# Top-k attention and a gated cosine feed-forward on one core: shared banks for scores and transposes, alternating feed-forward items, a shorter weight decode

## The chip, the cores and the metric

The kernel runs on one core of one Trainium2 chip. The core has TensorE (matrix products into the PSUM memory), VectorE, ScalarE and GpSimd (elementwise work), and SyncE, which here issues all DMA transfers. The metric is the device time of one launch in microseconds.

## The reference

For each of 8 batches and 8 heads, 576 queries of width 64 meet 576 keys. Only scores at or above the 32nd largest of a row take part in the softmax. The heads are put side by side to 4608 tokens of width 512, and a feed-forward block follows.

```python
scores = scale * np.matmul(q, k.transpose(0, 1, 3, 2))
kth = np.partition(scores, -top_k, axis=-1)[..., -top_k:-top_k + 1]
scores = np.where(scores >= kth, scores, -1000000000.0)
attn = np.exp(scores - np.max(scores, axis=-1, keepdims=True))
attn = attn / (np.sum(attn, axis=-1, keepdims=True) + 1e-09)
x = np.matmul(attn, v)          # then (B, H, S, D) -> (B*S, H*D)
h = x @ w_in                    # 512 -> 2048
out = (h * np.cos(h)) @ w_out   # 2048 -> 512
```

The weights arrive in 64-bit floating point; each is two 32-bit words, which the kernel turns into 32-bit floating point on the chip ("decoding").

## The kernel before

A **unit** is 128 tokens times one pair of heads; there are 36 x 4 = 144. For a unit, TensorE makes the scores (line 188) into the four PSUM banks of tag `sc`, and ScalarE copies them to the buffer `s` (line 198). VectorE finds the 32 largest of each row in four rounds of a MAX8 (line 212) for each head of the pair, with a replacement of the found values after the first three (line 215). GpSimd makes the bounds `nb` and `nd` from the largest and the 32nd (lines 222, 227), ScalarE masks with them (line 234) and takes exponentials with their row sums (line 242). GpSimd adds 1e-9 to the sums (line 249), VectorE takes the reciprocal (line 255), GpSimd normalises (line 260). TensorE transposes eight blocks of 128 x 128 (line 273) through two banks of tag `tp`, ScalarE copies them (line 274), a ninth, the tail, follows (lines 281, 282), and TensorE multiplies with the values (line 298), again into a `tp` bank. ScalarE puts the result into `xT`, the input of the feed-forward block (line 303).

The feed-forward block is cut into token blocks of 128 or 256. An **item** of the first product (`ff1`, line 344) gives 256 columns of `mm`; two fill a bank, four a `g` tile of 1024 columns. ScalarE evicts each bank (line 354). GpSimd reduces the argument of the cosine in three steps (lines 376 to 378) and a subtraction (line 385), ScalarE takes the sine (line 394), and GpSimd multiplies, the gate (line 401). In the last passes VectorE does GpSimd's part (lines 368, 371). An item of the second product (`ff2`, line 413) adds two of 16 slices of the hidden width; after eight items ScalarE evicts the bank (line 419) and SyncE writes 128 rows out. There are 288 items of each kind. Both products take their banks from tag `mm`, which has two.

Weights come in 32 chunks of 128 x 512, first 16 of `w_in`, then 16 of `w_out`. A chunk is loaded (line 102), taken apart by three ScalarE operations (lines 112 to 114), put together by three VectorE steps (lines 123, 124, 128), and finished by an addition and a multiplication on GpSimd (lines 131, 132).

The order of the work is written out by hand. The instructions of each engine run in the order of the program. The main loop (line 490) has one pass, a **slot**, per unit, and in slot `i` units `i` to `i - 3` are at different steps: `u` in its top-k rounds, `w` one unit behind in mask and exponentials, `x` two behind in normalising and transposes, `y` three behind in the product with the values. Scores are made one unit ahead. Feed-forward items are put between by `feed`, up to as many as a credit allows that grows by 4.3 a slot up to 6; it prefers the second product whenever the gates and all weights are ready. `decode` is called three times a slot, and a fourth time from slot 4 on. What is left of the feed-forward items after the last slot follows in a loop of its own (line 539). The first 12 units take their values one slot earlier.

## Time and profile before

| | us |
|---|---|
| median of 3 runs | 1827.48 (1827.01 to 1827.79) |
| the profiled execution | 1829.49 |
| its span, first to last instruction | 1827.4 |
| TensorE busy with products | 1614.0 (88%) |
| VectorE busy | 1492.9 (82%) |
| ScalarE busy | 1127.6 (62%) |
| GpSimd busy | 897.7 (49%) |

The mean granted clock of TensorE is 0.951 of full speed. "Busy" is the time in which an engine executes instructions; the product spans are partly modelled, and a busy TensorE may work at half the clock. A wait is put down to the engine and line that came last. In the rows, PE is TensorE, PEld its weight loads, DVE is VectorE, ACT is ScalarE, POOL is GpSimd, and L298 is line 298.

### The profile page before, as it was taken

To read this page: it belongs to the slowest core of one execution; us is meant where nothing else is said; L and a number is where in the kernel's file an instruction comes from. 1 tells how busy PE (TensorE), PEld (TensorE's weight loads), DVE (VectorE), ACT (ScalarE), POOL (GpSimd) and SP (SyncE) were. 2 spreads that over 40 slices of the span, in tenths; PEclk is the share of its full clock that TensorE was granted. 3 is DMA by queue.
4 is the path that set the end of the run, shared out by engine and by line. 5 is a ranking of instruction groups with operands and counts; after the bars stand their busy time and mean duration, and the time that the engine had idled before them with its cause. 6 is when DMAs were issued, how large, how long until landed. Compare 5 with 4: busy or idle time off the path is not lost.

```text
span 1827.4 us, 26780 instructions
## 1 busy us (share of the span) xinstructions
PE 1614.0 (88%) x9744; PEld 1098.3 (60%) x9744; DVE 1492.9 (82%) x3139; ACT 1127.6 (62%) x2022; POOL 897.7 (49%) x1128
## 2 busy tenths in 40 slices
PE   2464999899999898989899999999999999999997
PEld 1353757565747556565656566666666666666674
DVE  7999888989888889897979797879797978888421
ACT  5775575666665656666666666656666666667521
POOL 4787363363544536464646363645454545457200
PEclk9886999899999899999999999999999999999999
DMA  8430011002100020002000020001100010000000
GB/s 223 134 116 1 7 58 33 6 1 64 27 7 7 1 64 27 12 1 64 27 7 7 6 59 26 13 7 46 39 13 6 7 35 31 7 7 7 12 7 12
DMA packets 44227, 56.24 MB, mean 31 GB/s; under 512 B 10816, under 2 KB 27200, under 8 KB 44096
## 3 DMA queue, kind: packets, MB, share of 16 engines
q1 hardware_dynamic: 44096, 54.54, 9.9%
q8 instruction: 76, 1.25, 0.3%
q14 instruction: 55, 0.45, 0.1%
HBM read 45.09 MB, written 9.44 MB: 30 GB/s over the span
## 4 chain that ended last, share of the span: by engine, by line
PE 78%; ACT 8%; DVE 8%; POOL 3%; DMA 1%; issue 1%; SPq 0%; POOLq 0%; ACTq 0%
PE o L413 28%; PE mm L344 27%; PE o L298 9%; PE sc L188 8%; PE tp L273 5%; DVE m L212 2%; ACT x L394 2%; DVE rest L215 2%; ACT g L354 2%; ACT L394 1%; ACT pT L274 1%; POOL x L385 1%; ACT s L242 1%; PE tp L281 1%; DVE w_out L128 1%
## 5 line engine op out<-in xcount | busy, mean ns | idle before, releaser
L212 DVE MAX8 m<-rest 128x8 f32<-128x576 f32 x864 | 609.3, 747 | 0.0
L344 PE MATMUL mm<-xT,w_in 128*128 128x256 f32 (+1 forms) x2816 | 546.4, 346 | 25.0 <-ACT g L354 25.0
L413 PE MATMUL o<-w_out,g 128*128 128x512 f32 x1152 | 541.7, 612 | 17.5 <-POOL g L401 8.4
L344 PEld LDWEIGHTS mm<-xT,w_in 128*128 128x128 f32 x2816 | 447.4, 192 | 104.6 <-ACT g L354 38.4
L215 DVE MATCH_REPLACE8 rest<-m,rest 128x576 f32<-128x576 f32 x576 | 423.3, 742 | 0.0
L413 PEld LDWEIGHTS o<-w_out,g 128*128 128x128 f32 x1152 | 210.0, 194 | 267.5 <-issue 239.5
L249 POOL TENSOR_SCALAR den<-den 128x2 f32<-128x2 f32 x144 | 28.3, 196 | 667.6 <-ACT s L242 666.5
L212 DVE MAX8 m<-s 128x8 f32<-128x576 f32 x288 | 204.2, 750 | 129.6 <-ACT s L198 129.6
L234 ACT ACTIVATE s<-s,nb 128x576 f32<-128x576 f32 x288 | 207.9, 773 | 44.9 <-POOL nb L222 44.9
L354 ACT ACTIVATE g<-mm 128x512 f32<-128x512 f32 x144 | 85.4, 593 | 231.4 <-PE mm L344 231.4
L188 PE MATMUL sc<-k,q 64*128 64x288 f32 (+1 forms) x1280 | 201.5, 466 | 26.9 <-ACT s L198 15.8
L274 ACT COPY pT<-tp 128x512 f32<-128x512 f32 x288 | 153.8, 587 | 113.3 <-PE tp L273 113.2
L242 ACT ACTIVATE s<-s,nd 128x576 f32<-128x576 f32 x288 | 219.7, 765 | 0.5
L260 POOL TENSOR_SCALAR s<-s,rden 128x576 f32<-128x576 f32 x288 | 213.4, 752 | 0.4 <-DVE rden L255 0.4
L215 DVE MATCH_REPLACE8 rest<-m,s 128x576 f32<-128x576 f32 x288 | 211.6, 742 | 0.0
L273 PEld LDWEIGHTS tp<-ident,s 128*128 128x128 f32 x1152 | 137.8, 145 | 105.7 <-POOL s L260 53.8
L273 PE MATMUL tp<-ident,s 128*128 128x128 f32 x1152 | 157.6, 281 | 48.1 <-POOL s L260 45.2
L198 ACT COPY s<-sc 128x1152 f32<-128x1152 f32 x144 | 160.8, 1117 | 56.8 <-PE sc L188 56.6
L298 PE MATMUL o<-pT,v 128*64 128x128 f32 (+1 forms) x2560 | 179.9, 289 | 2.7 <-ACT pT L274 2.4
L298 PEld LDWEIGHTS o<-pT,v 128*64 128x64 f32 x2560 | 142.8, 150 | 58.5 <-ACT s L234 35.9
L401 POOL TENSOR_TENSOR g<-g,x 128x1024 f32<-128x1024 f32 x66 | 156.3, 2369 | 24.6 <-ACT x L394 24.6
L385 POOL TENSOR_TENSOR x<-g,x 128x1024 f32<-128x1024 f32 x66 | 156.6, 2373 | 5.3
(46 smaller groups left out, 1210.0 us busy)
## 6 DMA issues: line engine op xcount, KB each, us to landing
q<-in_q_dram SPq DMA_DIRECT2D x32, 288.0 KB, 3.1
out_dram<-ob SPq DMA_DIRECT2D x36, 256.0 KB, 2.0
st<-in_moe_w_in_dram SPq DMA_DIRECT2D x16, 512.0 KB, 5.2
v<-in_v_dram SPq DMA_DIRECT2D x32, 256.0 KB, 3.0
st<-in_moe_w_out_dram SPq DMA_DIRECT2D x16, 512.0 KB, 3.5
k<-in_k_dram SPq DMA_DIRECT2D x32, 144.0 KB, 3.3
k<-in_k_dram SPq DMA_DIRECT2D x32, 128.0 KB, 3.3
v_tail<-in_v_dram SPq DMA_DIRECT2D x64, 16.0 KB, 2.6
```

The costliest lines, as they stand in the source:

```text
L188: nc.tensor.matmul(sc[r0 : r0 + rows, j, h, 0:HS], st["q"][d, q0 : q0 + rows], st["k"][d, h * HS : (h + 1) * HS], start=True, stop=True,)
L212: nc.vector.max(m8[:, j, at], src[:, j])
L215: nc.vector.match_replace(rest[:, j], m8[:, j, at], src[:, j], NEG)
L234: nc.scalar.activation(out=s[:, j], in_=s[:, j], func=AF.Prelu, bias=nb[:, j, 1:2], scale=SCALE, alpha=FAR)
L242: nc.scalar.activation(out=s[:, j], in_=s[:, j], func=AF.Exp, bias=nd[:, j : j + 1], scale=1.0, accum_out=den[:, j : j + 1],)
L260: nc.gpsimd.tensor_scalar(out=s[:, j], in0=s[:, j], scalar1=rden[:, j : j + 1], scalar2=1.0, op0=ALU.mult, op1=ALU.mult,)
L273: nc.tensor.transpose(tp[:, c], s[:, j, k0 : k0 + P], ident)
L274: nc.scalar.copy(out=pT[:, :, j], in_=tp)
L298: nc.tensor.matmul(o[d, r], lhsT, rhs, start=c == 0, stop=c == NT)
L344: nc.tensor.matmul(mm[:, at : at + w], w_in[f // FC][:, c, (f % FC) * P : (f % FC + 1) * P], blk["xT"][:, c], start=c == 0, stop=c == NC - 1,)
L385: nc.gpsimd.tensor_tensor(out=x, in0=g, in1=x, op=ALU.subtract)
L413: nc.tensor.matmul(o, g[:, at : at + P], w_out[f], start=f == 0, stop=f == NF - 1)
```

## The change

The transposes of a unit go out together, the eight main ones into the four `sc` banks that the scores use, the tail into a bank `ot` that the product with the values uses as well; ScalarE copies all three afterwards. The second product has a bank `o2` of its own, so `mm` keeps its two for the first. `feed` alternates between the two kinds of items when both can go, with a credit of 3.7 a slot up to 5. Evictions of both products are not issued behind the last product of a bank but put on a list, which `take_banks` empties at two places of a slot. GpSimd's addition of 1e-9 becomes a VectorE operation ahead of the reciprocal, which moves to after round 2; normalising moves to the end of the slot before. Sines are taken only of tiles from an earlier slot. Chunks of weights are staged in the buffers of the `g` tiles (nine, not eight), taken apart in place, and decoded three a slot with two VectorE steps instead of three; GpSimd reads the staged words in place. An item waits only for the chunks that it needs. The first 8 units (before: 12) run their transposes and values early. In the main loop the loads of q, k and v stand behind the scores' copy, no longer at the start of the slot, `v` and `s` have a buffer less and `xT` one more, and the last two token blocks, not the last four, have 128 tokens. The diff, cut to its core:

```diff
-    CHUNKS, XB = 8, 4
...
-    def load_weights(i):
...
-        st = ffw.tile([P, CW, 2], I32, tag="x", name="st", bufs=XB)
...
-    def decode_first(i):
...
-        nc.scalar.activation(out=w, in_=hi.bitcast(F32), func=AF.Abs)
-        nc.scalar.sign(sg, hi)
-        nc.scalar.mul(out=r, in_=lo.bitcast(U32), mul=2.0**-29)
...
-    def decode_second(i):
...
-        nc.vector.tensor_scalar(out=w, in0=w, scalar1=2.0**-15, scalar2=None, op0=ALU.max)
-        nc.vector.tensor_scalar(
-            out=wi, in0=wi, scalar1=896 << 20, scalar2=3,
-            op0=ALU.bitwise_xor, op1=ALU.logical_shift_left,
-        )
-        nc.vector.tensor_scalar(
-            out=wi, in0=wi, scalar1=0x7FFFFFFF, scalar2=None, op0=ALU.bitwise_and
-        )
-        nc.gpsimd.tensor_tensor(out=wi, in0=wi, in1=r, op=ALU.add)
-        nc.gpsimd.tensor_tensor(out=w, in0=w, in1=sg, op=ALU.mult)
+    CHUNKS, XB = 9, 4
+    wq = {"next": 0, "loaded": deque(), "second": deque(), "done": 0, "ready": 0}
+
+    def load_weights(n):
+        for _ in range(n):
...
+            staging = len(wq["loaded"]) + len(wq["second"])
+            if staging >= 6 or staging + ff["live"] >= CHUNKS:
+                return
+            st = ffw.tile([P, CW, 2], I32, tag="g", name="st", bufs=CHUNKS)
+            nc.sync.dma_start(out=st.rearrange("p w i -> p (w i)"), in_=src)
+            wq["loaded"].append((st, dst))
+            wq["next"] = i + 1
+
+    def decode_first(n):
+
+
+        for _ in range(min(n, len(wq["loaded"]))):
+            st, w = wq["loaded"].popleft()
+            lo, hi = st[:, :, 0], st[:, :, 1]
+            nc.scalar.activation(out=w, in_=hi.bitcast(F32), func=AF.Abs, scale=2.0**16)
+            nc.scalar.sign(hi.bitcast(F32), hi)
+            nc.scalar.mul(out=lo, in_=lo.bitcast(U32), mul=2.0**-29)
+            wq["second"].append((st, w))
+
+    def decode_second():
+        for st, w in wq["second"]:
+            wi = w.bitcast(I32)
+            nc.vector.tensor_scalar(out=w, in0=w, scalar1=2.0, scalar2=None, op0=ALU.max)
+            nc.vector.tensor_scalar(
+                out=wi, in0=wi, scalar1=3, scalar2=None, op0=ALU.logical_shift_left
+            )
+
+    def decode_third():
+        while wq["second"]:
+            st, w = wq["second"].popleft()
+            wi = w.bitcast(I32)
+            nc.gpsimd.tensor_tensor(out=wi, in0=wi, in1=st[:, :, 0], op=ALU.add)
+            nc.gpsimd.tensor_tensor(out=w, in0=w, in1=st[:, :, 1].bitcast(F32), op=ALU.mult)
+            wq["done"] += 1
...
-        t = loads.tile([P, NT, P], F32, tag="v", name="v", bufs=6)
+        t = loads.tile([P, NT, P], F32, tag="v", name="v", bufs=5)
...
-        s = u["s"] = work.tile([P, 2, S], F32, tag="s", name="s", bufs=5)
+        s = u["s"] = work.tile([P, 2, S], F32, tag="s", name="s", bufs=4)
...
-    def add_eps(u):
-        den = u["den"]
-        nc.gpsimd.tensor_scalar(
-            out=den, in0=den, scalar1=1.0, scalar2=EPS, op0=ALU.mult, op1=ALU.add
-        )
-
     def reciprocal(u):
+        den = u.pop("den")
+        nc.vector.tensor_scalar(out=den, in0=den, scalar1=EPS, scalar2=None, op0=ALU.add)
         u["rden"] = small.tile([P, 2], F32, tag="rden", name="rden")
-        nc.vector.reciprocal(u["rden"], u.pop("den"))
+        nc.vector.reciprocal(u["rden"], den)
...
-    def transpose_main(u):
-
...
-        pT = u["pT"] = work.tile([P, NT, 2, P], F32, tag="pT", name="pT")
+    def transposes(u):
+
+        s = u.pop("s")
+        tp = u["tp"] = ps.tile([P, 2, 2, 512], F32, tag="sc", name="tp", bufs=1)
...
-            tp = ps.tile([P, NT, P], F32, tag="tp", name="tp")
-                nc.tensor.transpose(tp[:, c], s[:, j, k0 : k0 + P], ident)
-            nc.scalar.copy(out=pT[:, :, j], in_=tp)
-
-    def transpose_tail(u):
-
+                nc.tensor.transpose(
+                    tp[:, 0, j, c * P : (c + 1) * P], s[:, j, k0 : k0 + P], ident
+                )
+        tt = u["tt"] = ps.tile([P, 512], F32, tag="ot", name="tt", bufs=1)
+        nc.tensor.transpose(
+            tt[:, 0:P], s.rearrange("p j k -> p (j k)")[:, MAIN : MAIN + P], ident
+        )
+
+    def take_transposes(u):
+        tp, tt = u.pop("tp"), u.pop("tt")
+        pT = u["pT"] = work.tile([P, 2, NT * P], F32, tag="pT", name="pT")
+        for j in range(2):
+            nc.scalar.copy(out=pT[:, j], in_=tp[:, 0, j])
         pt = u["pT_tail"] = work.tile([P, P], F32, tag="pT_tail", name="pT_tail")
-        tp = ps.tile([P, 512], F32, tag="tp", name="tp")
-        s = u.pop("s").rearrange("p j k -> p (j k)")
-        nc.tensor.transpose(tp[:, 0:P], s[:, MAIN : MAIN + P], ident)
-        nc.scalar.copy(out=pt, in_=tp[:, 0:P])
+        nc.scalar.copy(out=pt, in_=tt[:, 0:P])
...
-        o = ps.tile([P, 512], F32, tag="tp", name="o")
+        o = u["o"] = ps.tile([P, 512], F32, tag="ot", name="o", bufs=1)
...
+
+    def take_values(u):
         blk = block_of[u["tok"]]
...
-        nc.scalar.copy(out=blk["xT"][:, u["hp"], at : at + P], in_=o[:, 0:P])
+        nc.scalar.copy(out=blk["xT"][:, u["hp"], at : at + P], in_=u.pop("o")[:, 0:P])
         blk["left"] -= 1
...
-    widths = [P] * 4 + [2 * P] * (B * S // (2 * P) - 4) + [P] * 4
+    widths = [P] * 4 + [2 * P] * (B * S // (2 * P) - 3) + [P] * 2
...
-        half = part // 2
+        full.append((take_first, blk, g, mm, part // 2))
+
+    def take_first(blk, g, mm, half):
         nc.scalar.mul(out=g[:, half * 512 : half * 512 + 512], in_=mm, mul=INV_2PI)
-        if half == 0:
-            return
-        fresh.append([blk, g])
+        if half == 1:
+            fresh.append([blk, g])
+
+    def take_banks():
+        while full:
+            take, *what = full.popleft()
+            take(*what)
...
-        if not waiting or (len(waiting) < least and waiting[0][3] + 2 > ff["now"]):
+        n = sum(c[3] < ff["now"] for c in waiting)
+        if n == 0 or (n < least and waiting[0][3] + 2 > ff["now"]):
             return
-        while waiting:
+        for _ in range(n):
...
-            blk["o"] = ps.tile([P, 512], F32, tag="mm", name="o2")
+            blk["o"] = ps.tile([P, 512], F32, tag="o2", name="o2", bufs=1)
...
+        full.append((take_second, blk, i, o))
+
+    def take_second(blk, i, o):
         ob = ffw.tile([P, DM], F32, tag="ob", name="ob")
         nc.scalar.mul(out=ob, in_=o, mul=2.0 * math.pi)
         row = blk["t0"] + i * P
         nc.sync.dma_start(out=out[row : row + P, :], in_=ob)
...
+    def can_first():
+        if not first:
+            return False
+        blk, i = first[0]
+        if blk["left"] or wq["ready"] < (((i + 1) * (256 // blk["w"]) - 1) // FC + 1) * NC:
+            return False
+        staging = len(wq["loaded"]) + len(wq["second"])
+        return i % 4 > 0 or ff["live"] + staging < CHUNKS
+
+    def can_second():
+        if not second:
+            return False
+        blk, i, f = second[0]
+        gated = sum(ff["tick"] >= t + 2 for t in blk["gated"])
+        return gated * 1024 // blk["w"] >= f + 2 and wq["ready"] >= NC * NF // FC + f + 2
+
     def feed(n):
 
         ff["tick"] += 1
         while n > 0 and ff["credit"] >= 1:
-            if second:
-                blk, i, f = second[0]
-                n_gated = sum(ff["tick"] >= t + 2 for t in blk["gated"])
-                if n_gated * 1024 // blk["w"] >= f + 2 and ff["weights"] == len(chunks):
-                    second.popleft()
-                    ff2(blk, i, f)
-                    n, ff["credit"] = n - 1, ff["credit"] - 1
-                    continue
-            if not first:
+            for kind in (ff["kind"], 1 - ff["kind"]):
+                if (can_first, can_second)[kind]():
+                    break
+            else:
                 return
-            blk, i = first[0]
-            need = (((i + 1) * (256 // blk["w"]) - 1) // FC + 1) * NC
-            if blk["left"] or ff["weights"] < need or (i % 4 == 0 and ff["live"] == CHUNKS):
-                return
-            first.popleft()
-            ff1(blk, i)
+            if kind == 0:
+                ff1(*first.popleft())
+            else:
+                ff2(*second.popleft())
+            ff["kind"] = 1 - kind
             n, ff["credit"] = n - 1, ff["credit"] - 1
-
...
-    for load, bufs, behind in ((load_qk, 5, -1), (load_v, 6, 4)):
+    for load, bufs, behind in ((load_qk, 5, -1), (load_v, 5, 3)):
         for n in range(NP, len(order)):
-            slot = last[order[n - bufs]] + behind if n >= bufs else 2
...
+    for hp in range(NP):
+        at_slot.setdefault(hp, []).append((load_v, 0, hp))
+    for hp in range(2, NP):
+        at_slot[hp - 2].append((load_qk, 0, hp))
+    EARLY = 2 * NP
     load_qk(0, 0)
-    load_weights(0)
+    load_weights(1)
+    load_qk(0, 1)
+    load_weights(2)
     scores(units[0])
     take_scores(units[0])
-    load_weights(1)
-    load_qk(0, 1)
-    scores(units[1])
-    decode()
-    take_scores(units[1])
-    for hp in range(2, NP):
-        load_qk(0, hp)
-    for hp in range(NP):
-        load_v(0, hp)
-    EARLY = 3 * NP
+    decode_first(3)
     for i in range(NU + 3):
         ff["end"] = i >= NU
         u, w, x, y = (units[i - n] if 0 <= i - n < NU else None for n in range(4))
+        early = w and i - 1 < EARLY
+        if x and i - 2 < EARLY:
+            x = None
+        if y and i - 3 < EARLY:
+            y = None
+        ff["credit"] = min(ff["credit"] + 3.7, 5.0)
+        ff["now"] += 1
+        wq["ready"] = wq["done"]
+        if w:
+            bounds(w)
+        if u:
+            if i > 0:
+                decode_second()
+            topk_round(u, 0)
+        take_banks()
+        if y:
+            values(y)
+        if i + 1 < NU:
+            scores(units[i + 1])
+        if y:
+            take_values(y)
+        if i + 1 < NU:
+            take_scores(units[i + 1])
         for load, b, hp in at_slot.get(i, []):
             load(b, hp)
-        ff["credit"] = min(ff["credit"] + 4.3, 6.0)
-        ff["now"] += 1
-        if w:
-            bounds(w)
-        if x:
-            normalise(x)
-        if u:
-            topk_round(u, 0)
-        decode()
+        gate(1)
         if w:
             mask(w)
             exponentials(w)
-        gate(1)
-        if w:
-            add_eps(w)
-        feed(1)
-        if y and i - 3 >= EARLY:
-            values(y)
-        if 0 < i < NU - 1:
-            scores(units[i + 1])
-            take_scores(units[i + 1])
+        if early:
+            reciprocal(w)
+            normalise(w)
         if u:
             topk_round(u, 1)
-        decode()
+            topk_round(u, 2)
+        if w and not early:
+            reciprocal(w)
+        feed(2)
+        take_banks()
+        if i > 0:
+            decode_third()
+            decode_first(3)
+        load_weights(3)
         reduce_first()
-        feed(2)
-        sines(2)
         if x:
-            transpose_main(x)
-        if u:
-            topk_round(u, 2)
-        decode()
+            transposes(x)
+            take_transposes(x)
+        feed(4)
+        if early:
+            transposes(w)
+            take_transposes(w)
+            values(w)
+            take_values(w)
         reduce_second()
-        feed(6)
-        if x:
-            transpose_tail(x)
-            if i - 2 < EARLY:
-                values(x)
+        if w and not early:
+            normalise(w)
         if u:
             topk_round(u, 3)
-        if i >= 4 and i < EARLY:
-            decode()
-        if w:
-            reciprocal(w)
-    while first or second:
+        sines(2)
+    while first or second or full:
         ff["now"] += 1
         ff["credit"] = 2.0
+        take_banks()
         gate(2)
         reduce_first()
         reduce_second()
```

## Rows read from the trace of the kernel before

**Rows 1.** Busy time by stretch, all engines: PE, PEld, DVE, ACT, POOL, clock, DMA.

```profile
8.65:193.84 185.19, 94.07 (x552) 68.37 (x553) 174.22 (x347) 118.97 (x219) 123.01 (x130) 0.82 0.36 107
193.84:415.02 221.18, 201.59 (x1436) 144.84 (x1435) 196.45 (x420) 140.22 (x260) 113.57 (x146) 0.93 0.08 24
415.02:1713.50 1298.48, 1214.16 (x7182) 813.41 (x7181) 1103.13 (x2353) 840.31 (x1497) 655.56 (x831) 0.97 0.07 22
1713.50:1827.40 113.90, 101.19 (x571) 69.92 (x569) 19.06 (x21) 25.68 (x46) 3.71 (x8) 0.97 0.03 10
```

**Rows 2.** The same of line 344 alone, then of line 413: PE, PEld, clock.

```profile
415.02:1713.50 1298.48, 408.98 (x1808) 320.43 (x1808) 0.97 0.07 22
1713.50:1827.40 113.90, 43.08 (x368) 42.26 (x368) 0.97 0.03 10
...
415.02:1713.50 1298.48, 424.65 (x902) 163.11 (x901) 0.97 0.07 22
1713.50:1827.40 113.90, 53.11 (x116) 21.75 (x114) 0.97 0.03 10
```

**Rows 3.** Timeline of PE over one slot: start us, us, engine, line.

```profile
1233.80 1.09 PE L298 MATMUL o<-pT,v 128*64 128x128 f32 x16
...
1236.21 3.70 PE L413 MATMUL o<-w_out,g 128*128 128x512 f32 x8
1239.75 1.04 PE L273 MATMUL tp<-ident,s 128*128 128x128 f32 x8
...
1244.31 1.89 PE L344 MATMUL mm<-xT,w_in 128*128 128x256 f32 x8
1246.14 1.09 PE L298 MATMUL o<-pT,v 128*64 128x128 f32 x16
```

**Rows 4.** Waits of 400 to 1700 us: us in total, times, longest.

```profile
DVE rden L255 <- POOL den L249: 88.2, 53, 6.1
...
PE tp L281 <- ACT pT L274: 52.6, 22, 4.3
...
PE mm L344 <- ACT g L354: 22.2, 36, 0.7
```

**Rows 5.** Busy time over two units that start without a wait.

```profile
318.24:337.64 19.40, 13.94 (x72) 8.95 (x71) 19.40 (x44) 14.32 (x24) 9.95 (x14) 0.60 0.00 0
```

**Rows 6.** Timeline of DVE, two decode steps.

```profile
129.98 0.42 DVE L123 TENSOR_SCALAR w_out<-w_out 128x512 f32<-128x512 f32 x1
...
136.62 2.44 DVE L128 TENSOR_SCALAR w_out<-w_out 128x512 int32<-128x512 int32 x1
```

**Rows 7.** Timeline of POOL over the same stretch.

```profile
134.97 1.33 POOL L132 TENSOR_TENSOR w_out<-w_out,lo_sg 128x512 f32<-128x512 f32 x1
136.26 2.52 POOL L385 TENSOR_TENSOR x<-g,x 128x1024 f32<-128x1024 f32 x1
```

**Rows 8.** Timeline of POOL in a slot at 801 us.

```profile
801.03 1.05 POOL L376 TENSOR_SCALAR x<-g 128x1024 f32<-128x1024 f32 x1 [0.29 <-ACT g L354]
...
804.43 2.36 POOL L385 TENSOR_TENSOR x<-g,x 128x1024 f32<-128x1024 f32 x1
...
807.21 1.48 POOL L260 TENSOR_SCALAR s<-s,rden 128x576 f32<-128x576 f32 x2
```

**Rows 9.** Timeline of ACT, mask and exponentials of one unit.

```profile
807.32 1.44 ACT L234 ACTIVATE s<-s,nb 128x576 f32<-128x576 f32 x2
...
808.78 1.28 ACT L242 ACT_TABLE_LOAD   x1
...
811.51 0.19 ACT L242 ACTIVATION_READ_ACCUMULATOR s<-s,nd 128x1 f32 x1
```

**Rows 10.** Costliest groups of the page: count, busy us, mean ns.

```profile
L354 ACT ACTIVATE g<-mm 128x512 f32<-128x512 f32 x144 | 85.4, 593 | 231.4 <-PE mm L344 231.4
...
L274 ACT COPY pT<-tp 128x512 f32<-128x512 f32 x288 | 153.8, 587 | 113.3 <-PE tp L273 113.2
...
L198 ACT COPY s<-sc 128x1152 f32<-128x1152 f32 x144 | 160.8, 1117 | 56.8 <-PE sc L188 56.6
```

More of the change, by code (lines that the diff above doesn't have):

```diff
@@ L90 @@
         chunks.append((moe_w_out[f * P : (f + 1) * P, :], w))
-    staged = {}
-    CHUNKS, XB = 8, 4
-    def load_weights(i):
-        if i >= len(chunks):
-            return
-        src, dst = chunks[i]
-        if not DECODE:
-            nc.sync.dma_start(out=dst, in_=src)
-            return
-        st = ffw.tile([P, CW, 2], I32, tag="x", name="st", bufs=XB)
-        nc.sync.dma_start(out=st.rearrange("p w i -> p (w i)"), in_=src)
-        staged[i] = [st]
-    def decode_first(i):
-        st = staged[i][0]
-        lo, hi = st[:, :, 0], st[:, :, 1]
-        w = chunks[i][1]
-        both = ffw.tile([P, 2, CW], F32, tag="g", name="lo_sg", bufs=CHUNKS)
-        r, sg = both[:, 0].bitcast(I32), both[:, 1]
-        nc.scalar.activation(out=w, in_=hi.bitcast(F32), func=AF.Abs)
-        nc.scalar.sign(sg, hi)
-        nc.scalar.mul(out=r, in_=lo.bitcast(U32), mul=2.0**-29)
-        staged[i] = [r, sg]
@@ new lines @@
+    ff = {"live": 0, "tick": 0, "now": 0, "credit": 0.0, "end": False, "kind": 0}
+    wq = {"next": 0, "loaded": deque(), "second": deque(), "done": 0, "ready": 0}
+    def load_weights(n):
+        for _ in range(n):
+            i = wq["next"]
+            if i >= len(chunks):
+                return
+            src, dst = chunks[i]
+            if not DECODE:
+                nc.sync.dma_start(out=dst, in_=src)
+                wq["next"] = wq["done"] = i + 1
+                continue
+            staging = len(wq["loaded"]) + len(wq["second"])
+            if staging >= 6 or staging + ff["live"] >= CHUNKS:
+                return
+            st = ffw.tile([P, CW, 2], I32, tag="g", name="st", bufs=CHUNKS)
+            nc.sync.dma_start(out=st.rearrange("p w i -> p (w i)"), in_=src)
+            wq["loaded"].append((st, dst))
+            wq["next"] = i + 1
@@ L294, in values @@
                     if c < NT:
-                        lhsT, rhs = st["v"][:, c, d], pT[:, c, j, r]
+                        lhsT, rhs = st["v"][:, c, d], pT[:, j, c * P + r0 : c * P + r0 + rows]
                     else:
@@ L318 @@
         t0 += w
-    ff = {"live": 0, "now": 0, "weights": 0, "credit": 0.0, "step": 0, "tick": 0, "end": False}
     first = deque((blk, i) for blk in blocks for i in range(2 * NF * blk["w"] // 512))
@@ L328 @@
     sined = deque()
+    full = deque()
     def ff1(blk, i):
```

23 lines of the change are left out of this document (3 added, 20 removed).

## The prediction

> **What bounds the kernel now.** The reading starts with busy time by stretch, cut where units 0, 12 and 32 start on VectorE and where unit 143 ends there [rows 1]. In the first stretch VectorE is busy 174.22 of 185.19 us and TensorE half of it: top-k search plus weight decoding is the limit, and TensorE lacks work. In the second TensorE is busy 201.59 of 221.18 us. In the third, 112 slots long, it is busy 1214.16 of 1298.48 us (93.5%) and VectorE 1103.13 (85%): TensorE sets the pace, 1298.48 / 112 = 11.59 us a slot. In the last only feed-forward work and the last units' attention are left. The granted clock is 0.82, 0.93, 0.97 and 0.97 of full speed (0.5 would be 1.2 GHz, 1.0 is 2.4 GHz), so TensorE loses time twice: idle, and then on the lower level.
>
> The second view counts feed-forward instructions in the last two stretches [rows 2]. Line 344 issues 16 to an item of a 128-token block and 8 to one of a 256-token block, line 413 issues 4. The last four blocks, of 128 tokens, have 512 of line 344, of which 368 lie in the last stretch; so the third holds 144 / 16 + (1808 - 144) / 8 = 9 + 208 = 217 items of the first product and 902 / 4 = 225 of the second: 442, or 3.95 a slot. The last holds 368 / 16 = 23 and 116 / 4 = 29: 52 items.
>
> The third view is TensorE's timeline over one slot without a wait, values to values [rows 3]: 1246.14 - 1233.80 = 12.34 us with four items of the second product and one of the first. Two of the second take 1239.75 - 1236.21 = 3.54 (1.77 each), one of the first 1246.14 - 1244.31 = 1.83. That leaves 12.34 - 7.08 - 1.83 = 3.43 us of attention (values, scores, transposes) in a slot. With 1.80 for a mean item, 3.95 items need 3.43 + 7.11 = 10.54 us where 11.59 are spent: about 1 us a slot, 118 over the stretch, is what can be won there.
>
> The waits of 400 to 1700 us name part of it [rows 4]: the tail transpose waits 52.6 us for the copy out of the main transposes' bank, the first product 22.2 us for its eviction. VectorE waits 88.2 us at the reciprocal. VectorE's own floor is a stretch of two units without idle time: 19.40 us, 9.70 a unit [rows 5].
>
> **The change part by part.** I price it by the same four stretches against the profiled execution (span 1827.4, its time 1829.49: 2.1 more). The median of the runs shown, 1827.48, is 2.0 under that execution, so a span that I work out stands nearly for a median as it is.
>
> Until unit 12. VectorE loses one decode step in three. A step takes 0.42 us at its fastest, and 2.44 where it starts during GpSimd's 2.52 us subtraction; a chunk's operation on GpSimd takes 1.33 [rows 6, 7]. The Trainium skill, SBUF — State Buffer, section "Who interferes with whom", says that a VectorE instruction in a two-port mode and GpSimd shut each other out of a shared port pair for a whole instruction. The trace agrees, with the 2.44 us. The new order puts six steps together at the start of a slot, when GpSimd may still add and multiply the chunks before. They cost 6 x 0.42 = 2.5 us at least and, each waiting for one chunk operation, 6 x 1.33 = 8.0 at most. I take 4.6, nearer the free row, since most of GpSimd's decoding lies beside the top-k rounds. A slot is then 9.70 + 4.6 = 14.3 us. Three chunks a slot (four were possible before) stretch decoding to slots 1 to 11. Unit 0 takes 9.7, a wait for the first weights 3, ten slots 143, one with two chunks 12.8. In slots 6 and 7 GpSimd's range reduction, 3.40 + 2.36 us [rows 8], stands between decoding and the next bounds; I let 4 us of each show, 8 together. ScalarE's nine decode operations in a row, ahead of the transposes' copies, may add 5. That is 181 us against 185.19: the saved step is largely spent on the slower rate of chunks. GpSimd's additions and multiplications now read every second word of the staged chunk, which no row shows: I take the old 1.33 us, nothing less, at most twice that, 8 us more of GpSimd a slot, of which some 5 would show. The bounds are 165 and 230.
>
> Units 12 to 31. Walking both queues through the new rules (credit 3.7 a slot, at most 5, nine buffers shared with staging, two ticks from gate to use) gives 20 items by slot 11 and 84 by slot 31: 64 items in 20 slots. TensorE needs 3.43 + 3.2 x 1.80 = 9.2 us a slot, less than VectorE's 9.70. Here VectorE is the bound. It gains the addition of 1e-9 that GpSimd did (128 x 2 elements), whose form no row shows: at least nothing, at most the 2.44 of a blocked step. GpSimd works about half the time, mostly in pieces of 1 to 2.4 us, so I take 0.4 on average. With 0.2 for uneven item supply a slot is 10.3: 206 us against 221.18, bounds 196 and 225.
>
> Units 32 to 143. The walk gives 494 items by slot 143: 410 in 112 slots, 3.66 each. TensorE needs 3.43 + 3.66 x 1.80 = 10.02, VectorE 9.70 + 0.4 = 10.1. Three waits of before lose their cause. All nine transposes go out together, so the tail no longer waits on the copy. The second product has its own bank, so both mm banks are free for the first while a sum is open. The reciprocal comes after round 2, by when the exponentials, early in ScalarE's slot, are through. What takes their place: the score banks now also hold the transposes, so scores wait for the transposes' copy and transposes for the scores' copy. Two items (3.6 us) cover the scores' copy of 1.12 us, as long as a slot has them; without them TensorE would pay it. From one values to the next, ScalarE's chain is 2.41 us (values and scores, 1233.80 to 1236.21), the scores' copy 1.12, mask to last accumulator read 4.38 (807.32 to 811.70, with a table load of 1.28; sines now come singly, so most slots have one), an eviction 0.59 and two copies 1.17 [rows 3, 9, 10]: 9.7 us, 0.3 under TensorE's slot. So a late mask is paid by TensorE.
>
> It is late where the range reduction waits for an eviction of the same slot. The accumulators then end at 2.41 + 1.12 + 3.10 (no load) = 6.6 us of the slot; eviction 0.59, reduction 3.40, subtraction 2.36, normalising 1.48 and bounds 0.42 (from 806.79 to 807.21) bring GpSimd to 14.9, which is 4.9 of the next slot [rows 8]. ScalarE was ready at 3.5 to 3.9, so the mask is 1.2 late, and 0.9 after the slack. A g tile comes every 2.2 slots, and in the walk some six in ten are such: 31 slots, 0.25 us on average. A slot is 10.1 + 0.3 = 10.4: 1165 us against 1298.48. Bounds: 9.9 and 11.4 a slot (the latter is the third rival).
>
> After unit 143. 576 - 494 = 82 items at 1.80 are 148 us, values and transposes of the last units 6. Before, 52 items (94 us) and some 6 us of attention took 113.9, so 14 us were lost. With items of both kinds alternating, 17 of the second product are left when the first runs out, 30 us of cover for the last gates. I take 6 us: 160, bounds 156 and 170. The late evictions cost nothing here or earlier: an eviction of 0.59 us has the next slot's values and scores ahead of its bank's reuse; without them TensorE would pay the 0.59. The loads move behind the scores' copy on the program's list but stay in order on SyncE's queue, where outputs and weights now stand ahead of them; a load into a q or k buffer waited for those same scores before, so I price the move at nothing. If it came later than the scores of the next slot, TensorE would wait.
>
> Sum: 8.65 (start to unit 0) + 181 + 206 + 1165 + 160 = 1721 us; I say 1722, 105 less than before.
>
> **The rivals.** A: nothing holds either engine in the long stretch. The slots run at TensorE's 10.0 us: 112 x 0.4 = 45 less, 1677. For it: VectorE's row at 9.70 without a break, and 0.3 us of slack in ScalarE's chain. Against it: blocked VectorE steps are in the trace.
>
> B: the moved addition is held behind GpSimd in most slots, as decode steps were, by half of the longest row, 1.2 us. VectorE then takes 9.70 + 0.1 + 1.2 = 11.0 a slot: 112 x 0.6 + 20 x 0.7 = 81 more, 1803. Against it: GpSimd is idle half the time. By the rule of the Trainium skill named above it can happen in any slot.
>
> C: slower. GpSimd becomes one chain with ScalarE: eviction 0.59, reduction 3.40, subtraction 2.36, normalising 1.48, bounds 0.42, mask to accumulator 4.38 make 12.6 us from one unit's exponentials to the next's [rows 8 to 10]. If every g tile meets it and nothing is caught up between, a slot averages (12.6 + 1.2 x 10.4) / 2.2 = 11.4: 112 more, 1834, slower than 1827.5. It decides from an average of 11.35 us on. Against it: in the slots between GpSimd has 3 to 4 us to spare.
>
> D: decoding gets slower: the six steps take 8.0 us, 10 x 3.4 = 34 more, or GpSimd's strided reads show 5 us in ten slots, 50 more: 1756 to 1772, still faster. Against it: GpSimd waits much in that stretch, 123 of 185 us busy [rows 1].
>
> **How the numbers follow.** The forecast gets 0.48, A 0.26, B 0.11, C 0.07, D 0.08. The range reaches from A with the early stretch at its lower bound (1677 - 16 = 1661) to just under B, 1800; left out are C, half of B and a little below A. 3.7 us, 0.2%, is about what a measurement of this kernel can tell from no change. Faster by more: 0.48 + 0.26 + 0.11 + 0.08 = 0.93, less 0.02 for cases of B that end at the old time: 0.91. Within: these 0.02. Slower: 0.07.
>
> **What would show it.** Right: units of the long stretch start 10.2 to 10.6 us apart on VectorE; the waits of the tail transpose and of line 344 for their copies are gone; TensorE is over 96% busy there at a granted clock near 1.0; about 160 us follow unit 143. Wrong: transposes or scores that wait for a ScalarE copy in most slots; the 128 x 2 addition with a mean near 1 us (B); the mask waiting for the bounds every second slot by 2 us or more (C); decode steps near 1.3 us or chunk operations near 2.6 (D).

## The result and the profile after

The changed kernel takes 1697.61 us (median of 4 runs, 1696.09 to 1698.95) against 1827.63 for the kernel before in the same comparison: a ratio of 0.9288, 95% interval 0.9272 to 0.9304. The forecast was 1722, with a range of 1661 to 1800. The profiled execution took 1698.95 us, its span is 1697.0, so spans again stand for medians within 2 us.

Busy time by stretch, cut at the same places (columns as in [rows 1], which these lines answer):

```profile
8.83:191.70 182.87, 106.66 (x667) 81.57 (x668) 172.27 (x327) 125.81 (x226) 128.72 (x122) 0.79 0.34 107
191.70:402.48 210.78, 187.57 (x1366) 133.06 (x1364) 200.31 (x442) 148.22 (x264) 104.72 (x125) 0.97 0.09 26
402.48:1543.70 1141.22, 1114.24 (x6932) 762.46 (x6932) 1120.76 (x2465) 856.03 (x1505) 605.89 (x705) 1.00 0.08 24
1543.70:1697.00 153.30, 147.97 (x653) 95.43 (x648) 30.25 (x31) 33.04 (x50) 3.59 (x5) 1.00 0.03 13
```

The stretches were forecast at 181, 206, 1165 and 160 us. Only the third is off by more than 7: 1141.22, or 10.19 a slot, where 10.4 was said. TensorE is busy 97.6% of it, VectorE 98.2%, at a granted clock of 1.00, the 2.4 GHz level (0.97 before).

The first and the second product's own lines, L355 then L431 [rows 2]:

```profile
402.48:1543.70 1141.22, 396.64 (x1656) 305.97 (x1656) 1.00 0.08 24
1543.70:1697.00 153.30, 63.61 (x392) 56.57 (x392) 1.00 0.03 13
...
402.48:1543.70 1141.22, 389.18 (x812) 146.29 (x812) 1.00 0.08 24
```

1656 / 8 + 812 / 4 = 410 items lie in the long stretch, as the walk of the queue said, 32 fewer than before. An item takes TensorE 1.78 us, the difference of two slots shown below. So the 157.3 us that this stretch lost divide in three: 32 x 1.78 = 57 are items put off to the tail (which grew by 39.4), 57 are idle time of TensorE (84.3 before, 27.0 now), and the other 43 are TensorE's own instructions. Some 29 of these are the clock: by the clock's records 65 us of the stretch's products ran at the lower level before and 7 us now, and from one product of line 413 to the next it is 853 ns there, 429 at the higher level. The last 14 were not traced.

The waits of 402 to 1543 us [rows 4]:

```profile
ACT s L243 <- POOL nb L231: 26.9, 28, 2.4
...
PE o L307 <- ACT pT_tail L291: 19.3, 21, 2.7
...
DVE den L258 <- ACT s L251: 16.2, 19, 1.2
...
PE tp L277 <- ACT s L207: 2.9, 2, 1.6
...
PE mm L355 <- ACT g L367: 0.3, 1, 0.3
```

The 52.6 us of the tail transpose and the 22.2 of the first product are gone (0.3 is left). Scores and transposes in common banks cost 2.9 us; no row has scores that wait for the transposes' copy. VectorE's wait at the softmax sums fell from 88.2 to 16.2.

TensorE's timeline, the starts of the values in four following slots [rows 3]:

```profile
750.85 1.09 PE L307 MATMUL o<-pT,v 128*64 128x128 f32 x16
...
759.62 1.09 PE L307 MATMUL o<-pT,v 128*64 128x128 f32 x16
...
771.38 0.88 PE L307 MATMUL o<-pT,v 128*64 128x128 f32 x12 [1.21 <-ACT pT_tail L291]
```

A slot with three items takes 759.62 - 750.85 = 8.77 us; the next, with four, 771.38 - 759.62 - 1.21 = 10.55 without its wait. VectorE's floor lies between the two, by its busy time over two units without a break [rows 5]:

```profile
710.88:730.69 19.81, 19.54 (x119) 12.90 (x116) 19.74 (x45) 15.75 (x27) 11.46 (x14) 1.00 0.04 14
```

That is 9.90 a unit, 0.20 over the old 9.70. From one unit's start on VectorE to the next there are 111 periods in the long stretch; 65 are at this floor (under 9.96) and 43 between 10 and 11. With the additions that were held (below) VectorE is busy 1120.76 / 112 = 10.01 us a slot, TensorE 1114.24 / 112 = 9.95: the two are nearly tied.

Two of the page's groups, the copies of scores and of transposes [rows 10]:

```profile
L207 ACT COPY s<-sc 128x1152 f32<-128x1152 f32 x144 | 161.2, 1120 | 127.4 <-PE sc L197 127.2
...
L289 ACT COPY pT<-tp 128x512 f32<-128x512 f32 x288 | 152.8, 582 | 17.4 <-PE tp L277 15.7
```

These copies cost what they did (1.12 and 0.58 us). Each waits mostly for TensorE's product.

### The profile page after: what moved, and what is told of

It is laid out like the page before. It is cut to its first block, busy times and chain, and to the rows that moved or that the text cites. A ratio compares the mean times of both kernels' runs of the same rounds, so it can differ in the third digit from the quotient of the medians.

```text
span 1697.0 us, 26520 instructions
## 1 busy us (share of the span) xinstructions
PE 1559.6 (92%) x9616; PEld 1074.2 (63%) x9616; DVE 1523.7 (90%) x3261; ACT 1165.5 (69%) x2046; POOL 844.8 (50%) x968
## 3 DMA queue, kind: packets, MB, share of 16 engines
q1 hardware_dynamic: 44096, 54.54, 10.4%
## 4 chain that ended last, share of the span: by engine, by line
PE 59%; ACT 16%; POOL 11%; DVE 11%; issue 2%; DMA 1%; SPq 0%; POOLq 0%; ACTq 0%
PE o L431 20%; PE mm L355 19%; PE o L307 8%; PE sc L197 8%; DVE m L221 5%; ACT s L251 5%; DVE rest L224 4%; PE tp L277 4%; ACT s L243 3%; POOL x L402 3%; ACT s L207 2%; POOL s L265 2%; ACT L251 2%; ACT pT L289 1%; POOL x L393 1%
## 5 line engine op out<-in xcount | busy, mean ns | idle before, releaser
L431 PE MATMUL o<-w_out,g 128*128 128x512 f32 x1152 | 548.5, 603 | 10.1 <-POOL g L419 7.0
L355 PE MATMUL mm<-xT,w_in 128*128 128x256 f32 (+1 forms) x2688 | 552.7, 353 | 0.3 <-ACT g L367 0.3
L355 PEld LDWEIGHTS mm<-xT,w_in 128*128 128x128 f32 x2688 | 446.9, 191 | 128.4 <-issue 89.8
L431 PEld LDWEIGHTS o<-w_out,g 128*128 128x128 f32 x1152 | 208.4, 191 | 197.5 <-issue 175.9
L307 PE MATMUL o<-pT,v 128*64 128x128 f32 (+1 forms) x2560 | 168.5, 277 | 55.8 <-ACT pT_tail L291 55.7
L307 PEld LDWEIGHTS o<-pT,v 128*64 128x64 f32 x2560 | 133.3, 142 | 133.9 <-ACT pT_tail L291 90.0
L197 PE MATMUL sc<-k,q 64*128 64x288 f32 (+1 forms) x1280 | 193.1, 449 | 11.6 <-DMA k<-in_k_dram 11.6
L277 PEld LDWEIGHTS tp<-ident,s 128*128 128x128 f32 x1152 | 138.2, 145 | 102.3 <-POOL s L265 52.6
L393 POOL TENSOR_SCALAR x<-g 128x1024 f32<-128x1024 f32 x63 | 66.2, 1050 | 205.8 <-ACT g L367 205.8
L314 ACT COPY xT<-o 128x128 f32<-128x128 f32 x144 | 37.9, 263 | 182.1 <-PE o L307 182.0
L419 POOL TENSOR_TENSOR g<-g,x 128x1024 f32<-128x1024 f32 x62 | 146.9, 2369 | 11.6 <-ACT x L412 11.6
L402 POOL TENSOR_TENSOR x<-g,x 128x1024 f32<-128x1024 f32 x63 | 149.3, 2370 | 5.3
```

The costliest lines, as they stand in the source:

```text
L197: nc.tensor.matmul(sc[r0 : r0 + rows, j, h, 0:HS], st["q"][d, q0 : q0 + rows], st["k"][d, h * HS : (h + 1) * HS], start=True, stop=True,)
L277: nc.tensor.transpose(tp[:, 0, j, c * P : (c + 1) * P], s[:, j, k0 : k0 + P], ident)
L307: nc.tensor.matmul(o[d, r], lhsT, rhs, start=c == 0, stop=c == NT)
L355: nc.tensor.matmul(mm[:, at : at + w], w_in[f // FC][:, c, (f % FC) * P : (f % FC + 1) * P], blk["xT"][:, c], start=c == 0, stop=c == NC - 1,)
L402: nc.gpsimd.tensor_tensor(out=x, in0=g, in1=x, op=ALU.subtract)
L431: nc.tensor.matmul(o, g[:, at : at + P], w_out[f], start=f == 0, stop=f == NF - 1)
```

## The experiments

All are edits of the changed kernel, run beside the kernel before. The slot is the mean of units 32 to 143, from VectorE's unit starts.

| kernel | us | ratio to before (95%) | slot, us |
|---|---|---|---|
| before | 1827.6 | 1 | 11.59 |
| after | 1697.6 | 0.9288 (0.9272 to 0.9304) | 10.19 |
| old banks | 1891.6 | 1.0346 (1.033 to 1.0361) | 11.58 |
| sum in `mm` | 1741.5 | 0.9523 (0.9509 to 0.9537) | 10.51 |
| second product first | 1765.5 | 0.966 (0.964 to 0.968) | 10.70 |
| credit 4.3 up to 6 | 1759.4 | 0.9619 (0.9599 to 0.9639) | 11.19 |
| credit 3.5 | 1755.6 | 0.9597 (0.9584 to 0.961) | 10.43 |
| credit 3.5, no addition | 1735.3 | 0.949 (0.9477 to 0.9503) | 10.23 |
| addition on GpSimd | 1722.3 | 0.9423 (0.941 to 0.9436) | 10.35 |
| three decode steps | 1711.8 | 0.9364 (0.935 to 0.9378) | 10.18 |
| evictions at once | 1705.1 | 0.9328 (0.9315 to 0.9342) | 10.22 |
| steps after round 0 | 1696.4 | 0.928 (0.9267 to 0.9292) | 10.18 |
| no addition | 1694.6 | 0.9272 (0.9259 to 0.9284) | 10.17 |
| no addition, steps after round 0 | 1692.4 | 0.9258 (0.9246 to 0.9271) | 10.18 |

**Which engine sets the pace?** The addition of 1e-9 is left out; the sums hold an exponential of zero, so they are 1 or more, and 1e-9 is lost in 32 bits anyway.

```diff
-        nc.vector.tensor_scalar(out=den, in0=den, scalar1=EPS, scalar2=None, op0=ALU.add)
```

> Leaves out the addition of 1e-9 to the row sums (the sums are at least 1). Theory M: in the long stretch (units 32 to 143, 10.19 us a unit after the change) VectorE's floor of 9.90 us and TensorE's need of 10.02 are nearly tied, and the addition, 0.15 us alone and up to 1.6 behind GpSimd, is what lifts VectorE over it. Without it VectorE's floor is 9.70, TensorE sets the pace at 10.05: 15 us less there, 5 in units 12 to 31, 2 before: about 1676 us against 1697.6. Rival T, TensorE or its chain with ScalarE sets the pace alone: 1693. Rival V, VectorE alone: its 39 us and the waits go in full, 1655.

Measured: 3 us less, near rival T (1693). VectorE's floor fell from 9.90 to 9.70 us, but the slot went from 10.19 to 10.17: the other slots became longer by what the short ones won (15 periods over 11 us, 2 in the changed kernel). TensorE, busy 9.95 and idle 0.24 a slot, sets the mean, and the theory of VectorE as the bound falls.

**The same with less work for TensorE.** Credit 3.5, with the addition and without:

```diff
-        ff["credit"] = min(ff["credit"] + 3.7, 5.0)
+        ff["credit"] = min(ff["credit"] + 3.5, 5.0)
```

> The changed kernel with one number altered: a slot's credit is 3.5 items, not 3.7. By the rules of the queue 390 items then fall into units 32 to 143 instead of 410, and 20 more follow unit 143. Theory: in the changed kernel TensorE paces the long stretch (9.95 us busy and 0.24 of waits a slot) with VectorE just under it (9.70 us and a mean of 0.27 for the moved addition, 9.97). With 20 items of 1.78 us less TensorE needs 9.63 + 0.24 = 9.87 a slot, so VectorE takes over at 9.97 to 10.05: 112 x 0.14 to 0.22 = 16 to 25 us are saved in the long stretch, 36 are added behind it, and the time is 1709 to 1718. Rival: VectorE's addition is hidden at any pace, slots follow TensorE down to 9.87, both ends cancel and the time stays within 1694 to 1702.

> The same credit of 3.5 and, besides, no addition of 1e-9 ahead of the reciprocal. Theory: without the addition VectorE needs 9.70 us a slot, TensorE's 9.87 sets the pace again, the long stretch saves about 36 us against the changed kernel and the tail adds 36: 1692 to 1699, that is 11 to 20 us under the kernel with the same credit and the addition (against 3 us at a credit of 3.7). Rival: the addition is hidden at this pace too, and the two kernels differ by 5 us at most.

Measured: the two differ by 20 us, at the upper end of what the theory said (11 to 20): at this rate VectorE's addition does show. But both are some 40 us slower than said. The long stretch of the first, with the addition:

```profile
400.70:1569.35 1168.65, 1103.15 (x6861) 751.00 (x6860) 1142.69 (x2465) 851.01 (x1499) 590.12 (x695) 0.98 0.08 23
```

By their instructions 393 items lie in it, 17 fewer than in the changed kernel. At 1.78 us they should have brought TensorE's busy time from 1114 to 1084; it is 1103. Some 15 of these 19 us are the clock (0.98; 37 us of products at the lower level, 7 in the changed kernel). TensorE idles 65.5 us, not 27. Waits in the stretch:

```profile
ACT s L243 <- POOL nb L231: 55.7, 48, 2.8
PE o L307 <- ACT pT_tail L291: 32.5, 27, 3.4
PE o L431 <- ACT ob L440: 26.2, 11, 4.2
```

The last two have grown by 38 us together, which is all the new idle time: the values wait longer, with 48 late masks and not 28, and the second product now waits for the eviction of its only bank (1.5 us in all in the changed kernel). VectorE is busy 1142.69 / 112 = 10.20 us a slot, 0.20 more than in the changed kernel, with as many instructions. The moved addition accounts for it, first here and then in the changed kernel's long stretch:

```profile
L258 DVE TENSOR_SCALAR den<-den 128x2 f32<-128x2 f32 x112 | 54.3, 485 | 22.1 <-ACT s L251 22.0
...
L258 DVE TENSOR_SCALAR den<-den 128x2 f32<-128x2 f32 x112 | 31.0, 277 | 16.6 <-ACT s L251 16.2
```

So the expectation was wrong in taking the changed kernel's waits (0.24 us a slot for TensorE, 0.27 for the addition) over to another rate. Whole numbers of items alone do not explain the miss. By the timeline 53 of the 112 slots have three items and 55 four. If three cost VectorE's floor of 9.90 and four TensorE's 10.55, the mean would be near 10.2. But from values to values TensorE takes 9.39 us for three and 11.23 for four, and the same sum would put the changed kernel (33 and 76 such slots) at 10.35, not 10.19: there a slot of three takes 9.07 us, so short slots do lend time to long ones. Why the waits grow at this rate was not traced further.

**More credit.**

```diff
-        ff["credit"] = min(ff["credit"] + 3.7, 5.0)
+        ff["credit"] = min(ff["credit"] + 4.3, 6.0)
```

> Credit 4.3 a slot up to 6 as before the change, everything else as after. Theory M: TensorE's work is the same in sum, so items that go earlier shorten the tail: slots of the long stretch take 10.6 to 10.7 us (TensorE alone sets the pace), the tail loses some 35 items of 1.8 us; the total stays within 10 us of 1697.6, between 1688 and 1708. Rival: the lower credit was the gain, as more items a slot bring back late masks and stalls: 1740 or more.

```profile
410.79:1663.67 1252.88, 1189.64 (x7108) 808.83 (x7109) 1114.11 (x2465) 844.58 (x1504) 637.22 (x724) 0.98 0.07 23
```

Measured: 62 us slower than the changed kernel. The long stretch is 112 us longer. By their instructions 444 items lie in it: the 34 that the tail no longer has (it is 57 shorter) are 60 of the 112, another 15 of TensorE's busy time go with the lower clock (0.98; 42 us of products at the lower level), and 36 are idle time (63.2 against 27.0). Units 12 to 31 add 9. A slot now gets anything from none to six items; by the queue's rules a higher credit empties the queue of finished gates and then waits for the next. VectorE waits for the softmax sums 86 times, not 19:

```profile
DVE den L258 <- ACT s L251: 134.9, 86, 6.2
```

The rival's number came, but not by late masks: there are 18 of them, fewer than the changed kernel's 28. Of the three rates run 3.7 is the best by far: 3.5 costs 58 us, 4.3 (with its cap of 6) costs 62.

**The banks.** The order of the changed kernel with the old banks: transposes, tail and values through the two of `tp`, the second product through `mm`.

```diff
-        tp = u["tp"] = ps.tile([P, 2, 2, 512], F32, tag="sc", name="tp", bufs=1)
+            tp = ps.tile([P, 512], F32, tag="tp", name="tp")
...
-        tt = u["tt"] = ps.tile([P, 512], F32, tag="ot", name="tt", bufs=1)
+        tt = u["tt"] = ps.tile([P, 512], F32, tag="tp", name="tt")
...
-        o = u["o"] = ps.tile([P, 512], F32, tag="ot", name="o", bufs=1)
+        o = u["o"] = ps.tile([P, 512], F32, tag="tp", name="o")
...
-            blk["o"] = ps.tile([P, 512], F32, tag="o2", name="o2", bufs=1)
+            blk["o"] = ps.tile([P, 512], F32, tag="mm", name="o2")
```

> As the run before, and the transposes go back into two banks of their own that the tail and the values share, as before the change; the order of the slot stays. Theory M: the tail transpose waits for the first copy again, about 1 us in each of 112 slots, so about 100 more than with only the sum moved: 1870. Rival: taking the score banks bought nothing by itself, since the order of the slot does the work: within 10 us of the run before.

```profile
DVE den L258 <- ACT s L251: 176.2, 94, 6.1
PE tt L283 <- ACT pT L291: 131.7, 110, 4.9
```

Measured: 194 us slower than the changed kernel, and slower than the kernel before. The tail transpose, now right behind the main ones, waits in 110 of 112 slots for the copy out of its bank; before it waited in 22, because items stood between [rows 4]. The new order needs the new banks; alone it is a loss.

Only the last of these edits, the second product back in `mm`:

> The second product's sum goes back into the two mm banks. Theory M: the bank of its own is what took TensorE's wait for evictions away. With the sum open most of the time, the first product has one bank, and since evictions are issued late it waits 1 to 2 us in about half of the slots: some 80 us more, about 1775, with the first product's wait for its eviction back in the list. Rival: the slack of TensorE and the alternation hide it: 1700.

```profile
DVE den L258 <- ACT s L251: 51.0, 41, 5.9
PE mm L355 <- ACT g L367: 30.2, 18, 4.3
```

Measured: 44 us slower, about halfway between the expectations. The first product waits for its evictions again, up to 4.3 us at a time where it was 0.7 before; that the evictions come later now would explain the longer ones, but this was not run apart. By difference the other 150 us of the test above belong to the places of the transposes, the tail and the values.

**Alternation.** The second product goes first whenever it can, as before the change:

```diff
-            for kind in (ff["kind"], 1 - ff["kind"]):
+            for kind in (1, 0):
```

> The second product is preferred again whenever it can go; no alternation. Theory M: the number of items a slot decides, not their kind; but a sum that ends and one that begins in the same feed share one bank and wait for a late eviction: 10 to 30 us more, 1708 to 1728. Rival: without alternation the last gates are not covered and first products come in bursts that wait for their two banks: 1750 or more.

```profile
DVE den L258 <- ACT s L251: 75.6, 53, 5.7
PE o L431 <- ACT ob L440: 39.8, 14, 4.8
```

Measured: 68 us slower, 57 of it in the long stretch and 11 behind unit 143. With sums back to back the one bank `o2` has to be evicted while TensorE wants it: 39.8 us of waits where the changed kernel has 1.5. The rival's bursts at the two `mm` banks cost only 3.4 us. At a credit of 3.7, alternation is what makes a single bank enough; at 3.5 the bank is waited for even so.

**Late evictions.** `take_banks()` behind every item:

```diff
             ff["kind"] = 1 - kind
+            take_banks()
```

> Evictions are issued right behind the item that fills a bank, no longer from the list. Theory M: ScalarE then stands before a product that TensorE has not finished, with the sines and the next slot's copies behind it; the mask starts later and TensorE pays in some slots: 20 us more, about 1717. Rival: ScalarE waits for TensorE at the scores anyway: within 5 us of 1697.6.

Measured: 7.5 us slower, between the two expectations. 4.8 of it lie in units 12 to 31, 3.2 in the long stretch.

**The place of the addition.** Back to GpSimd, behind the exponentials:

```diff
+            add_eps(w)
...
-        nc.vector.tensor_scalar(out=den, in0=den, scalar1=EPS, scalar2=None, op0=ALU.add)
```

> The addition of 1e-9 goes back to GpSimd, right behind the exponentials, as before the change; the reciprocal stays after round 2. Theory M: VectorE's floor falls to 9.70, but the reciprocal now waits for one more engine; 5 to 15 us less than 1697.6, between 1683 and 1693. Rival: moving the addition to VectorE was worth something by itself: 1710 or more, with the reciprocal waiting for GpSimd in most slots.

```profile
DVE rden L265 <- POOL den L258: 65.9, 61, 2.7
ACT s L243 <- POOL nb L231: 55.9, 44, 3.0
PE o L312 <- ACT pT_tail L296: 28.3, 30, 3.5
```

Measured: 25 us slower, and the way it takes shows a chain: the addition is late on GpSimd for VectorE's reciprocal in 61 slots, then the bounds (44 late masks, 28 in the changed kernel), then the values on TensorE (28.3 us, 19.3 in the changed kernel). Against the version without any addition, VectorE's costs 3 us and GpSimd's 28.

**The decode steps.** The old third step, an AND with 0x7FFFFFFF, put back:

```diff
+            nc.vector.tensor_scalar(
+                out=wi, in0=wi, scalar1=0x7FFFFFFF, scalar2=None, op0=ALU.bitwise_and
+            )
```

> A third VectorE step (an and with 0x7FFFFFFF, which changes nothing) is put back behind the two of each chunk. Theory M: VectorE is the bound until unit 12 and a step costs 0.86 us beside GpSimd: 32 x 0.86 = 27 us, of which 20 or more show: 1718 to 1725. Rival: the early stretch is held by GpSimd's and ScalarE's chains: within 5 us of 1697.6.

Measured: 14 us slower, 13.5 of it before unit 12, between the expectations. The 32 steps are 22.7 us of VectorE (77.9 in all against 55.2), so about three fifths of them showed.

The six steps behind top-k round 0 and not ahead of it:

```diff
         if u:
+            topk_round(u, 0)
             if i > 0:
                 decode_second()
-            topk_round(u, 0)
```

> The two VectorE decode steps of a slot's chunks are issued after top-k round 0, no longer before it. Theory M: the steps (mean 0.86 us after the change, 0.42 when free) are long because they meet GpSimd's chunk work of the slot before, which ends about when round 0 does. Their mean falls to about 0.5, VectorE loses 22 us of the 55 until unit 12, and half of that or more shows: about 1685. Rival: the early stretch is held by the chain of ScalarE's copies, products and exponentials: steps get shorter, the time stays within 3 us of 1697.6.

Two of its four groups of decode steps, on VectorE from 8 to 200 us:

```profile
L131 DVE TENSOR_SCALAR w_out<-w_out 128x512 int32<-128x512 int32 x16 | 15.3, 958 | 0.6
...
L130 DVE TENSOR_SCALAR w_in<-w_in 128x512 f32<-128x512 f32 x16 | 6.9, 434 | 0.0
```

Measured: the steps of `w_in` now run free (434 ns, 710 in the changed kernel), those of `w_out` do not; the mean of all is 0.69 us, not 0.5. VectorE saves 11 us, and the time moves by 1 us, inside its spread. VectorE's decoding is thus not alone in pacing the first slots. Together with the dropped addition the same edit gives the fastest version of all, 1692.4 us:

> Both edits together (the addition of 1e-9 left out, the decode steps after round 0). Theory M: they act in different stretches, so the gains add up: about 1664 us. Rival: the time won early is lost again at the end, as TensorE's work is the same: 1676, no more than without the addition alone.

Measured: 5 us under the changed kernel, all of it before unit 12 (177.5 us there, not 182.9), and neither 1664 nor 1676: both had counted on the 22 us that leaving out the addition did not give.

## Why the prediction was right, and where it was not

**The direction and the mechanism** held. The waits that were to vanish vanished, TensorE is 97.6% busy where over 96% was said, at a granted clock of 1.00, and the marks of rivals B, C and D are absent. Units of the long stretch start 10.19 us apart on average, just under the 10.2 to 10.6 of the forecast.

**Units 32 to 143: the one mis-sized term.** "A slot is 10.1 + 0.3" took VectorE (9.70 + 0.4 for the held addition) as the bound and put the late masks on top. Measured, TensorE is: 9.95 busy, where 10.02 was forecast, and 0.24 of waits, 10.19. The forecast itself says that TensorE pays for a late mask; put on TensorE's 10.02 its 0.25 would have given 10.27. The addition was over-sized: it adds 0.20 to VectorE's floor and takes 0.28 on average, not 0.4, and the no-addition kernel shows that leaving it out gains only 3 us; this stretch gets 2.3 us shorter. Two rows tell when it is held; VectorE first:

```profile
463.29 0.17 DVE L258 TENSOR_SCALAR den<-den 128x2 f32<-128x2 f32 x1 [0.48 <-ACT s L251]
...
485.25 1.19 DVE L258 TENSOR_SCALAR den<-den 128x2 f32<-128x2 f32 x1 [1.03 <-ACT s L251]
```

and GpSimd at the second of them:

```profile
484.06 2.35 POOL L402 TENSOR_TENSOR x<-g,x 128x1024 f32<-128x1024 f32 x1
```

The subtraction ends at 486.41, the addition at 486.44: two elements a row wait until the GpSimd instruction is over. The first addition ran while GpSimd was idle. The Trainium skill, SBUF — State Buffer, "Who interferes with whom", says that VectorE in a two-port mode and GpSimd exclude each other, and that the one that issues first keeps the shared ports for its whole instruction. The trace agrees, for a tile this small too. But the mean over 144 additions is 0.27 us:

```profile
L258 DVE TENSOR_SCALAR den<-den 128x2 f32<-128x2 f32 x144 | 39.1, 272 | 39.0 <-ACT s L251 38.5
...
L139 POOL TENSOR_TENSOR w_in<-w_in,st 128x512 int32<-128x512 int32 x16 | 21.7, 1359 | 0.0
L140 POOL TENSOR_TENSOR w_in<-w_in,st 128x512 f32<-128x512 f32 x16 | 20.9, 1307 | 1.3
```

So rival B (1.2 us in most slots) fails. The last two groups are GpSimd's chunk operations on strided words, 1.31 to 1.36 us on average where the old ones took 1.27 to 1.29 (the 1.33 of [rows 7] was a long one): rival D's 2.6 is far off.

**The late masks** were right in number, 28 where 31 were walked, but not in size: 18 are of 0.4 us or less and ten of 2.0 to 2.4, where 1.2 was said for all. That their mean, 0.96, comes near it is luck. One of the long ones, GpSimd first, then ScalarE:

```profile
527.81 2.36 POOL L402 TENSOR_TENSOR x<-g,x 128x1024 f32<-128x1024 f32 x1
530.15 1.47 POOL L265 TENSOR_SCALAR s<-s,rden 128x576 f32<-128x576 f32 x2
531.59 0.20 POOL L231 TENSOR_SCALAR nb<-m 128x4 f32<-128x4 f32 x1
```

```profile
531.83 1.44 ACT L243 ACTIVATE s<-s,nb 128x576 f32<-128x576 f32 x2 [2.06 <-POOL nb L231]
```

That is the chain the forecast described: subtraction, normalising, bounds, mask [rows 8, 9]. It arrives at TensorE as the wait of the values, 19.3 us where 28 were said: 14 of the 28 late masks are followed by such a wait some 6 us later, 15 us in all, and the other waits of the values have another cause that was not traced. In rival C this is the same chain in every second slot; it came in one of four, and GpSimd caught up between. Rival A (1677) erred about as far as the forecast, to the other side: it had the pace of TensorE right and left out its 0.24 of waits.

**Until unit 12** the sum, 181 for 182.87, is right by errors that cancel. Slots 1 to 5 take 15.3 us where 14.3 was said, with steps of 0.86 us on average (0.77 was priced). Some on VectorE:

```profile
107.28 0.42 DVE L130 TENSOR_SCALAR w_out<-w_out 128x512 f32<-128x512 f32 x1
107.74 1.39 DVE L131 TENSOR_SCALAR w_out<-w_out 128x512 int32<-128x512 int32 x1
109.05 1.50 DVE L130 TENSOR_SCALAR w_out<-w_out 128x512 f32<-128x512 f32 x1
110.59 1.15 DVE L131 TENSOR_SCALAR w_out<-w_out 128x512 int32<-128x512 int32 x1
```

and on GpSimd beside them:

```profile
107.38 1.47 POOL L139 TENSOR_TENSOR w_out<-w_out,st 128x512 int32<-128x512 int32 x1
108.92 1.35 POOL L140 TENSOR_TENSOR w_out<-w_out,st 128x512 f32<-128x512 f32 x1
110.25 1.21 POOL L393 TENSOR_SCALAR x<-g 128x1024 f32<-128x1024 f32 x1
```

The first step is free; each of the next three ends 0.28 us after the GpSimd instruction beside it, so the 64 steps take 55.2 us where the old 96 took 59.9. Against that, decoding was through a slot earlier: unit 11 takes 9.91 us, not 12.8. "The saved step is largely spent" is borne out: the stretch is 2.3 us shorter than before, though without the saving it is 13.5 longer. But it is spent on longer steps (0.86 us, 0.62 before), not "on the slower rate of chunks".

**Units 12 to 31 and the tail** came at 210.78 (206) and 153.3 (160). The tail lost hardly any of the 6 us kept for last gates: 82 items at 1.78 and 6 of attention are 152. **The late evictions**, "nothing here or earlier", are worth 7.5 us of gain. The moved loads were priced at nothing; no run here tests that alone, nor the new places of the reciprocal, the normalising and the sines, the buffer counts, the block widths or the 8 early units. Whether the credit alone would have helped the kernel before wasn't tried.

## What to carry to other kernels

A set of edits to a hand-written order is one design: banks, alternation, credit and the addition's place are worth 194, 68, 62 and 25 us when each is taken back alone, more in sum than the 130 the whole change gave. So their prices cannot be added, and the new order with the old banks is slower than the kernel before. A wait measured at one rate of work does not hold at another: with 3.5 items a slot and not 3.7, the addition took 54.3 us and not 31.0, late masks came 48 times and not 28, and the single bank cost 26.2 us and not 1.5. And on an engine that is only just not the bound, ask first what a removed instruction would uncover: the same addition was worth 3 us at one rate of items and 20 at another.

## What was not expected of the hardware

A VectorE operation on 128 x 2 elements took from 0.15 to 1.61 us in the changed kernel, and up to 1.93 with a credit of 3.5, by what GpSimd ran beside it. GpSimd's operations on every second 32-bit word cost nearly what contiguous ones do (1.31 to 1.36 us on average against 1.27 to 1.29).
